# A gated mix of segment attention and a GLU on one core: token gates as VectorE row sums, the second x tile by transposing DMAs, other first loads, the last tile in halves, and a new order

## The chip, the core and the metric

The kernel runs on one core of a Trainium2 chip. The metric is the device time of one execution in microseconds (us). TensorE is called PE, VectorE DVE, ScalarE ACT, GpSimd POOL, SyncE SP.

## What is computed

Input x has 2048 tokens of 512 features in bfloat16. The result mixes two branches by a gate that each token has:

```python
g = sigmoid((x * gate_w).sum(-1, keepdims=True))   # one gate per token
a = A(x)      # 32 heads of 16, 4 segments of 512 tokens: causal softmax attention inside a segment,
              # plus a linear memory of the segments before it (phi(q) @ M, / phi(q) @ z), mixed by
              # sigmoid(beta) per head, then @ wo
b = (gelu(x @ w_gate) * (x @ w_up)) @ w_down        # inner width 1792
out = g * a + (1 - g) * b
```

## The kernel before

All weights stay in SBUF. The work goes by segments s = 0 to 3 of 512 tokens. Each piece of work is a task with a name; its instructions belong to one engine. The list `ORDER` at the end of the file holds all names in one sequence, written out by hand; each engine runs its own tasks in the order of that list and waits for data, with semaphores that the `Emitter` derives from what each instruction reads and writes. A digit behind a colon is the PSUM bank (four banks of 512 float32 columns, `psD`), a letter `a` or `d` says whether ACT or DVE empties the bank. An engine never overtakes: what stands behind a waiting instruction waits too. SP's queue, which issues nearly all DMAs, is such a sequence as well.

The names, with s the segment and t a quarter of the 512 features or of the tokens:
- `ld_x0_*` load the natural x of segment 0; `xtr` turns 128x128 blocks of it on PE and `xev` empties them into `xT` (feature on the partition; three buffers). Segment 1 goes the same way; segments 2 and 3 come as transposing DMAs (`ld_x2_*`, `ld_x3_*`, four each, line 343).
- `K`, `Q`, `V` are projections (four 128x128 by 512 matmuls each, line 452), with `Kev`, `Qev`, `Vev` emptying them and `kpada`, `kpadb` laying K out in halves.
- `st` fills the four banks `psX` with scores (line 586); a segment has 18 fills, lettered A to E; `exp` (ACT, line 592) turns them into `pt`, `msk` (POOL) applies the mask; `pv` multiplies with V (line 628); `tp`, `pvp`, `ot` (DVE) turn, scale and turn back into `oT`.
- `vsh` and `ktr` are DMAs that shift V between partition halves and turn phi(K); `phk`, `phq` make phi; `mz`, `mzacc` write the memory, `nz`, `nd`, `nzp`, `ndp` read it.
- `G`, `U` are the GLU's two projections (14 blocks each), emptied by `Gev` and `gelu` or by `gd` (ACT) and `h` (DVE, line 690); `out` is the down projection (line 703), `wo` the output projection (line 715); `wev` scales the former by 1 - g, `oev` (line 718) adds the latter times g, `dma` stores a tile of 128 tokens. `ost` and `wds` have two buffers each.
- The gates: `gate_w` is loaded as four rows, turned on PE (`gwtr`) and copied (`gwev`). `gate{s}` is 16 matmuls of one column each (line 427) into a bank; `gz` clamps, `gr` takes the exponential, `go` makes g and 1 - g (`gtok`, `omgt`).

At the start, `warm1` runs eight matmuls on zeros. The queues then hold, on SP: x0's first half, the first half of `wk`, `wq` in two halves, `gate_w`, `wv`, x1 in halves, `w_gate` in halves, `beta`; on ACT: x0's second half and the second half of `wk`.

Of the kernel before, what the change touches and what calls it, by code (L numbers as in the profile page):

```python
# [246 lines left out]
def _build(es, nc, A_x, A_wq, A_wk, A_wv, A_wo, A_beta, B_w_gate, B_w_up, B_w_down, gate_w, out):  # L247
# [173 lines left out]
    def gates(s):  # L421
        sl = Slot()
        c = slice(4 * s, 4 * s + 4)
        mm = []
        for q in range(4):
            for kb in range(4):
                mm.append(I(lambda e, q=q, kb=kb: e.matmul(
                    BK[sl.i][:, q:q + 1], xT[s % R_XT][:, kb, q * 128:(q + 1) * 128], gatew[:, kb:kb + 1],
                    start=(kb == 0), stop=(kb == 3)), [("xT", s % R_XT, kb), ("gatew",)], [bk(sl)]))
# [262 lines left out]

    def outputs(s):
        for qt in range(4):
# [19 lines left out]
            so = Slot()  # L714
            one(f"wo{s}_{qt}", PE, 4 * T_MM, [I(lambda e, kb=kb, q=q, so=so: e.matmul(  # L715
                BK[so.i][:, :], oT[:, kb, q], wo[:, kb, :], start=(kb == 0), stop=(kb == 3)),
                [("oT", kb), ("wo",)], [bk(so)]) for kb in range(4)], opens=True)
            one(f"oev{s}_{qt}", DVE, 0.66, [I(lambda e, so=so, gt=gt, wi=wi, oi=oi: e.scalar_tensor_tensor(  # L718
                out=ost[oi][:, :], in0=BK[so.i][:, :], scalar=gtok[:, gt:gt + 1], in1=wds[wi][:, :],
                op0=ALU.mult, op1=ALU.add), [bk(so), ("gtok", s), ("wds", wi)], [("ost", oi)])])  # L720
            one(f"dma{gt}", SP, 0.5, [I(lambda e, gt=gt, oi=oi: e.dma_start(out[0, gt * 128:(gt + 1) * 128, :], ost[oi][:, :]),
                                        [("ost", oi)], [("out", gt)], dma_sem=sem(f"s_out{gt}"))], lat=2.0)

    def head_gates():
# [7 lines left out]
        one("gwtr", PE, T_TR, [I(lambda e: e.transpose(BKbf[sg.i][:, 0:4], gw4, ident[0:4, 0:4]),
                                 [("gw4",), ("omem", 0), ("ident",)], [bk(sg)])], opens=True, bias=30.0)
# [196 lines left out]
```

## Time and profile before

| | |
|---|---|
| runs | 274.26, 274.30, 274.33 us (median 274.3) |
| span of the profiled execution, first to last instruction | 272.5 us |
| profiled execution's own time | not given beside its span; the runs lie 1.8 us above the span |
| granted TensorE clock | 1.000 |
| PE, DVE, ACT, POOL busy | 265.6, 210.4, 206.6, 98.9 us |
| gate matmuls on PE, line 427 | 64, in four blocks |
| turns of x on PE, line 759 | 32 |
| landing of `wk`, first and second half | 6.45 us, 7.16 us |
| first K matmul | 6.54 us |
| read from HBM, written | 8.66 MB, 2.10 MB |

Busy time is the time in which an engine has at least one instruction under way. Matmuls overlap in the array, so PE's busy time says little; starts of consecutive matmuls say more. The chain of waits follows the last instruction back to whatever released each step. A DMA's landing is the time at which its semaphore is raised. All times count from the first instruction.

### The profile page before, as it was taken

How to read it: one execution, taken by the hardware profiler on the slowest of the kernel's cores; microseconds unless marked ns; L12 is line 12 of the kernel's file. 1: busy time of each engine (PE TensorE's matmuls, PEld its weight loads, DVE VectorE, ACT ScalarE, POOL GpSimd, SP SyncE). 2: the span in 40 equal slices, each digit the busy share in tenths (PEclk: the TensorE clock that was granted, in tenths of full speed). 3: DMA queues.
4: the chain of work that ended last, by engine and by line, in shares of the span. 5: the costliest groups of instructions: out<-in, count | busy, mean ns of one | idle time of the engine just before them, and what ended most of it. 6: DMA issues, size and time to landing. Idle time of an engine off the chain costs nothing.

```text
span 272.5 us, 6260 instructions
## 1 busy us (share of the span) xinstructions
PE 265.6 (97%) x2641; PEld 115.5 (42%) x2641; DVE 210.4 (77%) x398; ACT 206.6 (76%) x171; POOL 98.9 (36%) x151
## 2 busy tenths in 40 slices
PE   6999999989999999999999999999999999999995
...
GB/s 230 276 152 182 122 221 156 0 4 33 0 117 158 30 19 19 2 4 19 0 2 2 67 53 0 2 61 61 22 4 0 0 2 2 22 19 2 39 2 78
DMA packets 21812, 14.90 MB, mean 55 GB/s; under 512 B 11800, under 2 KB 20760, under 8 KB 21784
## 3 DMA queue, kind: packets, MB, share of 16 engines
...
q14 instruction: 7, 0.06, 0.1%
HBM read 8.66 MB, written 2.10 MB: 39 GB/s over the span
## 4 chain that ended last, share of the span: by engine, by line
PE 85%; DVE 11%; DMA 2%; issue 1%; ACT 0%; ACTq 0%
PE psD L452 46%; PE psD L703 16%; PE psX L586 8%; PE psD L628 6%; PE psD L715 5%; DVE gb L690 2%; DMA wk<-in_A_wk_dram 2%; DVE ob L639 1%; PE psD L553 1%; DVE phk L466 1%; PE psD L533 1%; PE psD L522 1%; DVE oT L647 1%; DVE phq L466 1%; DVE ob L645 1%
## 5 line engine op out<-in xcount | busy, mean ns | idle before, releaser
L592 ACT ACTIVATE pt<-psX 128x2048 bf16<-128x2048 f32 x72 | 135.1, 1877 | 36.9 <-PE psX L586 35.7
L598 POOL TENSOR_TENSOR pt<-pt,ctri 128x256 bf16<-128x256 bf16 x128 | 94.4, 742 | 157.5 <-ACT pt L592 142.4
L452 PE MATMUL psD<-xT,wu 128*128 128x512 bf16 x224 | 54.8, 380 | 0.7 <-DVE gb L690 0.7
L452 PE MATMUL psD<-xT,wg 128*128 128x512 bf16 x224 | 53.2, 380 | 0.3 <-DVE kT L446 0.3
L703 PE MATMUL psD<-wd,gb 128*128 128x512 bf16 x224 | 53.2, 380 | 0.1
L690 DVE TENSOR_TENSOR gb<-psD,gb 128x512 bf16<-128x512 f32 x56 | 37.4, 681 | 10.3 <-PE psD L452 10.1
L507 DVE STREAM_TRANSPOSE tT<-psD 128x512 f32<-128x512 f32 x47 | 32.3, 703 | 10.1 <-PE psD L628 6.7
L452 PEld LDWEIGHTS psD<-xT,wg 128*128 128x128 bf16 x224 | 21.0, 98 | 26.0 <-issue 1.5
L703 PEld LDWEIGHTS psD<-wd,gb 128*128 128x128 bf16 x224 | 20.6, 98 | 25.4 <-issue 2.6
L452 PEld LDWEIGHTS psD<-xT,wu 128*128 128x128 bf16 x224 | 20.0, 98 | 26.5 <-issue 3.2
L586 PE MATMUL psX<-qT,kD 32*128 32x192 bf16 (+7 forms) x512 | 28.6, 287 | 0.0
L639 DVE SCALAR_TENSOR_TENSOR ob<-tT,gq,rc 128x256 bf16<-128x256 f32 x32 | 18.4, 575 | 1.1
L628 PE MATMUL psD<-pt,vnat 64*17 64x128 bf16 (+7 forms) x512 | 18.9, 283 | 0.0
L586 PEld LDWEIGHTS psX<-qT,kD 32*128 32x128 bf16 x512 | 8.3, 92 | 24.8 <-issue 9.3
L628 PE MATMUL psD<-pt,vsh 64*17 64x128 bf16 (+7 forms) x512 | 18.2, 283 | 0.0
L452 PE MATMUL psD<-xT,wk 128*128 128x512 bf16 x64 | 16.5, 380 | 1.4 <-DMA wk<-in_A_wk_dram 1.3
L673 ACT ACTIVATE gb<-psD 128x512 bf16<-128x512 f32 x28 | 15.2, 597 | 2.1 <-PE psD L452 1.9
L452 PE MATMUL psD<-wv,xT 128*128 128x512 bf16 x64 | 16.5, 380 | 0.0
L452 PE MATMUL psD<-xT,wq 128*128 128x512 bf16 x64 | 16.3, 380 | 0.0
L715 PE MATMUL psD<-wo,oT 128*128 128x512 bf16 x64 | 16.1, 380 | 0.0
L718 DVE SCALAR_TENSOR_TENSOR ost<-psD,gtok,wds 128x512 bf16<-128x512 f32 x16 | 11.9, 742 | 5.3 <-PE psD L715 4.8
L628 PEld LDWEIGHTS psD<-pt,vnat 64*17 64x17 bf16 x512 | 11.5, 86 | 9.0 <-issue 5.5
...
## 6 DMA issues: line engine op xcount, KB each, us to landing
...
```

Of the source, the lines that this page charges most:

```text
L452: one(name, PE, n * T_MM, [I(lambda e, i=i: e.matmul(BK[sl.i][:, :], lhs(i), rhs(i), start=(i == 0), stop=(i == n - 1)), reads(i), [bk(sl) ...
L507: one(f"tp{name}", DVE, 0.605, [I(lambda e, sl=sl, ti=ti: e.transpose(tT[ti][:, :], BK[sl.i][:, :]), [bk(sl)], [("tT", ti)])], bias=bias)
L586: ins.append(I(lambda e, t=t, kb=kb, ncol=ncol, c0=c0, g=g: e.matmul(XALL[:, g * 512 + c0:g * 512 + c0 + ncol], kD[b][32 * g:32 * g + 32, ...
L592: one(f"exp{s}_{name}", ACT, 2048 * 0.000833 + 0.05, [I(lambda e: e.activation(pt[slot][:, :, :], xin, ACTF.Exp, scale=ATT_SCALE), [("X",) ...
L598: ins.append(I(lambda e, mv=mv: e.tensor_tensor(mv, mv, cm, ALU.mult), [("pt", slot), ("causal",)], [("pt", slot)]))
L628: ins.append(I(lambda e, kb=kb, slot=slot, c0=c0, n=n, g=g, r0=r0, sl=banks[j], va=va: e.matmul(BK[sl.i][32 * g:32 * g + 17, 64 * kb:512], ...
L639: I(lambda e, ti=ti, ri=ri, t=t, j=j, dst=dst: e.scalar_tensor_tensor(out=dst, in0=t_rows(ti), scalar=gq[:, 2 * t + j:2 * t + j + 1], in1= ...
L673: t = one(f"gd{s}_{ft}", ACT, 0.485, [I(lambda e, gi=gi, f=f, sl=sl: e.activation(gb[gi][:, f, :], BK[sl.i][:, :], ACTF.Gelu_apprx_tanh), ...
L690: one(f"h{s}_{ft}", DVE, 0.605, [I(lambda e, sl=sl, gi=gi, f=f: e.tensor_tensor(gb[gi][:, f, :], BK[sl.i][:, :], gb[gi][:, f, :], ALU.mult ...
L703: mm.append(I(lambda e, fb=fb, gi=gi, f=f, q=q, sl=sl: e.matmul(BK[sl.i][:, :], gb[gi][:, f, q], wd[:, fb, :], start=(fb == 0), stop=(fb = ...
L715: one(f"wo{s}_{qt}", PE, 4 * T_MM, [I(lambda e, kb=kb, q=q, so=so: e.matmul(BK[so.i][:, :], oT[:, kb, q], wo[:, kb, :], start=(kb == 0), s ...
L718: one(f"oev{s}_{qt}", DVE, 0.66, [I(lambda e, so=so, gt=gt, wi=wi, oi=oi: e.scalar_tensor_tensor(out=ost[oi][:, :], in0=BK[so.i][:, :], sc ...
```

## The change

- Gates: instead of PE matmuls over `xT`, DVE multiplies natural x by `gate_w`, laid out on all partitions (`gwb`), and sums along the row: two instructions with an accumulated output for each half segment (`gs`), then `gm` clamps. Segment 0 takes the natural x that is in SBUF; the others load it again in halves (`ld_n`) into one buffer `xn`. `gwtr`, `gwev` and the gate matmuls are gone.
- Segment 1 of x comes by four transposing DMAs, which wait for `wv`; its natural load, its turns and its evictions are gone.
- First loads: `wk` in four quarters and `wq` in two halves, alternating between SP's queue and ACT's. The turns of x0 are split by halves of its rows (`xp`).
- K of segment 0 is made two column blocks at a time, with the input block outermost.
- A small exponential (`table`) on ACT at the start.
- The last tile of 128 tokens goes through `wo`, `oev` and `dma` in two column halves, by way of `junk`.
- The whole list is another sequence, with other banks and other engines for some evictions (`wev`: 6 on DVE and 10 on ACT instead of 12 and 4).

The diff, cut; of the list only the start, one middle part and the end are shown:

```diff
...
-    gatew = sb("gatew", [P, 4])
+    gwb = sb("gwb", [P, 512])
+    xn = sb("xn", [P, 2, 512])
+    junk = sb("junk", [P, 512])
+    gzr = sb("gzr", [P, 16], F32)
     betab = sb("betab", [P, 8])
...
-    gw4, ball = omem[0:4, 0, 0:P], omem[:, 1, 0:H]
-    stage = (R_PT - 1, R_PT - 2)
+    ball = omem[:, 1, 0:H]
+    stage = R_PT - 1
...
-    def ld_xt(s):
+    def ld_xt(s, wait):
         for kb in range(4):
             load(f"x{s}_{kb}", SP, lambda e, kb=kb: e.dma_start_transpose(
                 xT[s % R_XT][:, kb, :], A_x[0, s * 512:(s + 1) * 512, kb * 128:(kb + 1) * 128]),
-                [("xT", s % R_XT, kb)], issue=1.31, lat=3.0, wait=[("ld", "wo")], ranked=False)
-
-    def ld_xp(s, h, eng, wait=()):
-        ld_w(f"x{s}_{h}", eng, pt[stage[s]][:, halves[h], :],
-             A_x[0, s * 512:(s + 1) * 512, :].rearrange("(q p) d -> p q d", p=P)[:, halves[h], :],
-             [("xs", s, h)], 0.25, wait)
-
-    ld_xp(0, 0, SP)
-    ld_xp(0, 1, ACT)
-    ld_w("wk0", SP, wk[:, halves[0], :], wsrc(A_wk)[:, halves[0], :], [("wk", 0)], 0.25)
-    ld_w("wk1", ACT, wk[:, halves[1], :], wsrc(A_wk)[:, halves[1], :], [("wk", 1)], 0.25)
-    ld_w("wq0", SP, wq[:, halves[0], :], wsrc(A_wq)[:, halves[0], :], [("wq", 0)], 0.25)
-    ld_w("wq1", SP, wq[:, halves[1], :], wsrc(A_wq)[:, halves[1], :], [("wq", 1)], 0.25)
-    ld_w("gw", SP, gw4, gate_w.rearrange("(kb p) -> kb p", p=P), [("gw4",)], 0.01, ["x0_0"])
+                [("xT", s % R_XT, kb)], issue=1.31, lat=3.0, wait=[("ld", wait)], ranked=False)
+
+    for h, eng in ((0, SP), (1, ACT)):
+        ld_w(f"x0_{h}", eng, pt[stage][:, halves[h], :],
+             A_x[0, 0:512, :].rearrange("(q p) d -> p q d", p=P)[:, halves[h], :], [("xs", h)], 0.25)
+    for kb, eng in ((0, SP), (1, ACT), (2, SP), (3, ACT)):
+        ld_w(f"wk{kb}", eng, wk[:, kb, :], wsrc(A_wk)[:, kb, :], [("wk", kb)], 0.125)
+    for h, eng in ((0, SP), (1, ACT)):
+        ld_w(f"wq{h}", eng, wq[:, halves[h], :], wsrc(A_wq)[:, halves[h], :], [("wq", h)], 0.25)
     ld_w("wv", SP, wv[:], wsrc(A_wv), [("wv",)], 0.5, ["x0_1"])
     ld_w("beta", SP, ball, A_beta.partition_broadcast(P), [("ball",)], 0.02, ["wk0"])
-    ld_xp(1, 0, SP, ["wk0", "wk1"])
-    ld_xp(1, 1, SP, ["wq0"])
-    ld_w("wg0", SP, wg[:, halves[0], :], wgr[:, halves[0], :], [("wg", 0)], 0.9, ["wq1"])
-    ld_w("wg1", SP, wg[:, halves[1], :], wgr[:, halves[1], :], [("wg", 1)], 0.9, ["wv"])
-    ld_w("wu0", SP, wu[:, halves[0], :], wur[:, halves[0], :], [("wu", 0)], 0.9, ["x1_1"])
-    ld_w("wu1", SP, wu[:, halves[1], :], wur[:, halves[1], :], [("wu", 1)], 0.9, ["wg0"])
-    ld_w("wd0", SP, wd[:, 0:HFT, :], wdr[:, 0:HFT, :], [("wd", 0)], 0.9, ["wg1"])
+    ld_w("gwb", SP, gwb[:, :], gate_w.partition_broadcast(P), [("gwb",)], 0.125, ["wk0"])
+    ld_w("wg0", SP, wg[:, halves[0], :], wgr[:, halves[0], :], [("wg", 0)], 0.9, ["wk3"])
+    ld_w("wg1", SP, wg[:, halves[1], :], wgr[:, halves[1], :], [("wg", 1)], 0.9, ["wq0"])
+    ld_xt(1, "wv")
+    ld_w("wu0", SP, wu[:, halves[0], :], wur[:, halves[0], :], [("wu", 0)], 0.9, ["wg0"])
+    ld_w("wu1", SP, wu[:, halves[1], :], wur[:, halves[1], :], [("wu", 1)], 0.9, ["wg1"])
+    ld_w("wd0", SP, wd[:, 0:HFT, :], wdr[:, 0:HFT, :], [("wd", 0)], 0.9, ["x1_3"])
     ld_w("wd1", SP, wd[:, HFT:NFT, :], wdr[:, HFT:NFT, :], [("wd", 1)], 0.9, ["wu0"])
     ld_w("wo", SP, wo[:], wsrc(A_wo), [("wo",)], 0.5, ["wu1"])
-    ld_xt(2)
-
+    ld_xt(2, "wo")
...
+    one("table", ACT, 1.3, [I(lambda e: e.activation(rcm[:, 0:8], warm[:, 0:8], ACTF.Exp), [("warm",)], [("rcm",)])])
...
     def gates(s):
-        sl = Slot()
         c = slice(4 * s, 4 * s + 4)
-        mm = []
-        for q in range(4):
-            for kb in range(4):
-                mm.append(I(lambda e, q=q, kb=kb: e.matmul(
-                    BK[sl.i][:, q:q + 1], xT[s % R_XT][:, kb, q * 128:(q + 1) * 128], gatew[:, kb:kb + 1],
-                    start=(kb == 0), stop=(kb == 3)), [("xT", s % R_XT, kb), ("gatew",)], [bk(sl)]))
-        one(f"gate{s}", PE, 0.45, mm, opens=True, bias=30.0)
-        one(f"gz{s}", DVE, 0.2, [I(lambda e: e.tensor_scalar(gz[:, c], BK[sl.i][:, 0:4], ZMAX, None, ALU.min),
-                                   [bk(sl)], [("gz", s)])], bias=30.0)
+        for h in range(2):
+            xs, k = (pt[stage][:, halves[h], :], ("xs", h)) if s == 0 else (xn[:, :, :], ("xn",))
+            if s > 0:
+                ld_w(f"n{s}_{h}", SP, xn[:, :, :],
+                     A_x[0, s * 512:(s + 1) * 512, :].rearrange("(q p) d -> p q d", p=P)[:, halves[h], :],
+                     [("xn",)], 0.25, ["wo"])
+            one(f"gs{s}_{h}", DVE, 1.4, [I(lambda e, q=q, xs=xs: e.scalar_tensor_tensor(
+                out=junk[:, :], in0=xs[:, q % 2, :], scalar=1.0, in1=gwb[:, :], op0=ALU.mult, op1=ALU.mult,
+                accum_out=gzr[:, 4 * s + q:4 * s + q + 1]), [k, ("gwb",), *([("pt", stage)] if s == 0 else [])],
+                [("junk",), ("gzr", s, q)]) for q in (2 * h, 2 * h + 1)])
+        one(f"gm{s}", DVE, 0.2, [I(lambda e: e.tensor_scalar(gz[:, c], gzr[:, c], ZMAX, None, ALU.min),
+                                   [("gzr", s, q) for q in range(4)], [("gz", s)])])
         one(f"gr{s}", ACT, 0.2, [I(lambda e: e.activation(gr[:, c], gz[:, c], ACTF.Exp), [("gz", s)], [("gr", s)])],
             bias=30.0)
         one(f"go{s}", DVE, 0.6, [
...
     def project(s):
         b, b3 = s % 2, s % R_XT
+        if s == 0:
+            kb2 = {}
+            for t in (0, 1):
+                kb2[t], kb2[t + 2] = pair = Slot(), Slot()
+                one(f"K0_{t}", PE, 8 * T_MM, [I(lambda e, t=t + 2 * j, i=i, sl=pair[j]: e.matmul(
+                    BK[sl.i][:, :], wk[:, i, t * 128:(t + 1) * 128], xT[0][:, i, :], start=(i == 0), stop=(i == 3)),
+                    [("xT", 0, i), ("wk", i)], [bk(pair[j])]) for i in range(4) for j in range(2)], opens=True)
         for t in range(4):
-            sl = dense(f"K{s}_{t}", lambda i, t=t: wk[:, i, t * 128:(t + 1) * 128], lambda i: xT[b3][:, i, :],
-                       lambda i: [("xT", b3, i), ("wk", i // 2)], 4)
+            sl = kb2[t] if s == 0 else dense(f"K{s}_{t}", lambda i, t=t: wk[:, i, t * 128:(t + 1) * 128], lambda i: xT[b3][:, i, :],
+                       lambda i: [("xT", b3, i), ("wk", i)], 4)
             evict(f"Kev{s}_{t}", kT[:, t, :], sl, [], [("kT", 0, t)])
             kin = kT[:, t, :].rearrange("p (m c) -> p m c", c=64)
...
             one(f"h{s}_{ft}", DVE, 0.605, [I(lambda e, sl=sl, gi=gi, f=f: e.tensor_tensor(
                 gb[gi][:, f, :], BK[sl.i][:, :], gb[gi][:, f, :], ALU.mult), [bk(sl), ("g", gi, f)], [("g", gi, f)])])
+    outs = []
+
     def outputs(s):
         for qt in range(4):
             gt = 4 * s + qt
...
                 (DVE, 0.66, [I(lambda e, sl=sl, gt=gt, wi=wi: e.tensor_scalar(
                     wds[wi][:, :], BK[sl.i][:, :], omgt[:, gt:gt + 1], None, ALU.mult),
                     [bk(sl), ("omgt", s)], [("wds", wi)])])], L_DVE)
...
+            parts = (("", slice(0, 512)),) if gt < 15 else (("a", slice(0, 256)), ("b", slice(256, 512)))
+            for pi, (sfx, c) in enumerate(parts):
+                so, w = Slot(), c.stop - c.start
+                one(f"wo{s}_{qt}{sfx}", PE, 4 * T_MM / len(parts), [I(lambda e, kb=kb, q=q, so=so, c=c, w=w: e.matmul(
+                    BK[so.i][:, 0:w], oT[:, kb, q], wo[:, kb, c], start=(kb == 0), stop=(kb == 3)),
+                    [("oT", kb), ("wo",)], [bk(so)]) for kb in range(4)], opens=True)
+                dst, dk = (ost[oi], ("ost", oi)) if not sfx else (junk, ("junk", pi))
+                one(f"oev{s}_{qt}{sfx}", DVE, 0.66, [I(lambda e, so=so, gt=gt, wi=wi, dst=dst, c=c, w=w: e.scalar_tensor_tensor(
+                    out=dst[:, c], in0=BK[so.i][:, 0:w], scalar=gtok[:, gt:gt + 1], in1=wds[wi][:, c],
+                    op0=ALU.mult, op1=ALU.add), [bk(so), ("gtok", s), ("wds", wi), *([("junk",)] if sfx else [])], [dk])])
+                outs.append(f"s_out{gt}{sfx}")
+                one(f"dma{gt}{sfx}", SP, 0.5, [I(lambda e, gt=gt, dst=dst, c=c: e.dma_start(
+                    out[0, gt * 128:(gt + 1) * 128, c], dst[:, c]), [dk], [("out", gt, pi)],
+                    dma_sem=sem(outs[-1]))], lat=2.0)
     def head_gates():
...
-        sg = Slot()
-        one("gwtr", PE, T_TR, [I(lambda e: e.transpose(BKbf[sg.i][:, 0:4], gw4, ident[0:4, 0:4]),
-                                 [("gw4",), ("omem", 0), ("ident",)], [bk(sg)])], opens=True, bias=30.0)
-        one("gwev", DVE, 0.1, [I(lambda e: e.tensor_copy(gatew[:, :], BKbf[sg.i][:, 0:4]), [bk(sg)], [("gatew",)])],
-            bias=-150.0)
...
-    def turn_x(s):
-        xs = pt[stage[s]]
-        for kb in range(4):
-            sl = Slot()
-            one(f"xtr{s}_{kb}", PE, 4 * T_TR, [I(lambda e, q=q, kb=kb, sl=sl: e.transpose(
-                BKbf[sl.i][:, q * 128:(q + 1) * 128], xs[:, q, kb * 128:(kb + 1) * 128], ident[:, :]),
-                [("xs", s, q // 2), ("pt", stage[s]), ("ident",)], [bk(sl)]) for q in range(4)], opens=True)
-            task(f"xev{s}_{kb}", [
-                (ACT, 0.477, [I(lambda e, kb=kb, sl=sl: e.activation(xT[s][:, kb, :], BKbf[sl.i][:, 0:512], ACTF.Copy),
-                                [bk(sl)], [("xT", s, kb)])]),
-                (DVE, 0.335, [I(lambda e, kb=kb, sl=sl: e.tensor_copy(xT[s][:, kb, :], BKbf[sl.i][:, 0:512]),
-                                [bk(sl)], [("xT", s, kb)])])], L_DVE)
-
-    turn_x(0)
-    turn_x(1)
+    for kb in range(4):
+        sl = Slot()
+        for h in range(2):
+            one(f"xp{kb}_{h}", PE, 2 * T_TR, [I(lambda e, q=q, kb=kb, sl=sl: e.transpose(
+                BKbf[sl.i][:, q * 128:(q + 1) * 128], pt[stage][:, q, kb * 128:(kb + 1) * 128], ident[:, :]),
+                [("xs", h), ("pt", stage), ("ident",)], [bk(sl)]) for q in (2 * h, 2 * h + 1)], opens=(h == 0))
+        task(f"xev0_{kb}", [
+            (ACT, 0.477, [I(lambda e, kb=kb, sl=sl: e.activation(xT[0][:, kb, :], BKbf[sl.i][:, 0:512], ACTF.Copy),
+                            [bk(sl)], [("xT", 0, kb)])]),
+            (DVE, 0.335, [I(lambda e, kb=kb, sl=sl: e.tensor_copy(xT[0][:, kb, :], BKbf[sl.i][:, 0:512]),
+                            [bk(sl)], [("xT", 0, kb)])])], L_DVE)
+
     head_gates()
     for s in range(NSEG):
         if s == NSEG - 1:
-            ld_xt(s)
+            ld_xt(s, "wo")
         project(s)
         if s > 0:
             memory_read(s)
...
-            for gt in range(16):
-                e.wait_ge(sem(f"s_out{gt}"), 16)
+            for name in outs:
+                e.wait_ge(sem(name), 16)
...
 ORDER = """
...
-ld_x0_0 ld_x0_1 ld_wk1 warm0 ident consts causal1 causal0 masks warm1:0 ld_wk0 ld_wq1 ld_wq0 ld_gw ld_wv ld_x1_0
-ld_x1_1 ld_wg1 ld_wg0 ld_beta xtr0_2:1 xtr0_3:2 xtr0_1:3 xtr0_0:0 vones0 xev0_3:d xev0_2:a xev0_1:a xev0_0:d K0_0:1
-Kev0_0:d K0_2:2 kpada0_0 kpadb0_0 Q0_0:3 Qev0_0:a Kev0_2:a gwtr:0 K0_1:1 st0_0A exp0_0A V0_2:3 K0_3:2 gwev Kev0_1:d
-kpada0_1 Kev0_3:a xtr1_1:0 V0_1:1 st0_0B Vev0_2:d phka0_0 exp0_0B phkb0_0 kpada0_3 xev1_1:d phka0_2 Vev0_1:d Q0_2:3
...
-pv3_3:12 wev3_0:d wev3_1:a tp3_d31 tp3_d30 pvp3_31 pvp3_30 ot3_3 dma10 dma11 out3_2_0:3 out3_3_0:0 out3_3_1 out3_3_2
-wo3_0:2 wo3_1:1 oev3_0 oev3_1 dma12 dma13 out3_2_1 out3_2_2 wo3_2:2 wo3_3:1 wev3_2:d wev3_3:a oev3_2 oev3_3 dma14
-dma15
+ident warm0 warm1:0 ld_x0_0 ld_x0_1 ld_wk0 ld_wk2 xp1_0:1 xp0_0:2 xp3_0:3 xp0_1 masks causal0 consts causal1 xp3_1
+xp2_0:0 ld_wk1 ld_wk3 ld_wq0 ld_wq1 xev0_3:a xev0_0:d xp2_1 xp1_1 xev0_1:d xev0_2:a K0_0:23 ld_beta ld_wv Kev0_0:d
+kpada0_0 table K0_1:10 Kev0_1:a Kev0_2:a ld_gwb Q0_0:2 kpadb0_0 betab Q0_1:1 gs0_0 Qev0_0:a Kev0_3:a kpadb0_2 phka0_2
+st0_0A exp0_0A V0_2:3 V0_0:2 Q0_3:0 vones0 gs0_1 causal Vev0_0:d kpadb0_1 Qev0_1:d st0_0B Vev0_2:a exp0_0B phkb0_2
+ld_wg0 ld_x1_1 ld_wg1 Q0_2:3 V0_3:2 G0_2:1 st0_0C exp0_0C Qev0_3:d Qev0_2:d kpada0_2 Gev0_2:d phkc0_2 phka0_0 phkb0_0
+ld_x1_2 ld_x1_0 ld_x1_3 V0_1:0 V1_1:3 G0_0:1 Vev1_1:d Vev0_3:d kpadb0_3 kpada0_1 Gev0_0:d st0_0D Q1_3:3 G0_1:2 V1_2:1
+Vev0_1:a phkc0_0 exp0_0D st0_0E Qev1_3:d ktr0_2 ld_wu1 vsh0_01 Vev1_2:d G1_5:0 K1_2:3 Kev1_2:d G0_3:1 kpada1_2
+Gev0_3:d Gev1_5:d Gev0_1:a exp0_0E bexp gph st0_1A vsh0_21 vsh0_00 exp0_1A G1_4:2 V1_0:3 K1_0:1 msk0_0C msk0_0A
...
+exp1_0D st1_0E exp1_0E out0_1_2 wo0_1:3 V2_3:0 wev0_1:d gs1_1 gm1 oev0_1 nzp1 st1_1A out0_2_0:1 out0_2_1 wo0_0:2
+out0_2_2 G1_8:3 oev0_0 wev0_2:d ndp1_1 phka2_0 Vev2_3:d G1_13:2 exp1_1A G1_10:1 G1_7:0 gelu1 gd1_13 gd1_8 gd1_10 gd1_7
+G1_9:2 nd1_2:3 gd1_9 msk1_0D ndp1_0 ld_n2_0 vsh1_20 ktr1_2 tp1_m2 ndp1_2 phka2_2 vsh1_21 ld_x3_1 st1_1B msk1_1A
+msk1_0E dma0 dma1 vsh1_01 ld_x3_0 msk1_0C msk1_0A pv1_0:10 exp1_1B V2_2:2 out0_3_0:3 tp1_d00 Vev2_2:d tp1_d01 U1_9:1
...
+wev2_2:a st3_3B msk3_2A msk3_2D msk3_2E msk3_2C pv3_2:12 tp3_d20 pvp3_11 wo2_2:3 out3_1_0:0 exp3_3B msk3_3B st3_3C
+exp3_3C go3 tp3_d21 ot3_0 out3_1_1 out3_1_2 out3_0_0:1 st3_3D pvp3_21 ot3_1 oev2_2 pvp3_20 dma11 dma10 msk3_3A msk3_3C
+out3_0_1 out3_0_2 exp3_3D wev3_1:a msk3_3D out3_2_0:2 pv3_3:30 ot3_2 wev3_0:d out3_3_0:1 out3_2_1 out3_2_2 out3_3_1
+tp3_d30 pvp3_30 tp3_d31 pvp3_31 ot3_3 wo3_0:3 oev3_0 dma12 wo3_1:0 out3_3_2 oev3_1 wev3_2:a dma13 wo3_3a:3 wev3_3:a
+oev3_3a dma15a wo3_2:2 oev3_2 dma14 wo3_3b:0 oev3_3b dma15b
```

More of the change, by code (lines that the diff above doesn't have):

```diff
@@ L713, in outputs @@
                     [bk(sl), ("omgt", s)], [("wds", wi)])])], L_DVE)
[L714 to L722, printed above, removed]
+            parts = (("", slice(0, 512)),) if gt < 15 else (("a", slice(0, 256)), ("b", slice(256, 512)))
[12 more added lines that the diff above has]
+                    dma_sem=sem(outs[-1]))], lat=2.0)
     def head_gates():
@@ L841 @@
-st0_0D Qev0_1:a Vev0_0:a betab Vev0_3:d kpadb0_3 kpadb0_1 G1_5:2 Q1_3:0 G0_0:3 Gev1_5:d Qev1_3:d Gev0_0:d exp0_0D bexp
-phkb0_2 st0_0E exp0_0E vsh0_21 ld_wu1 vsh0_00 vsh0_01 vsh0_20 Q0_3:2 Qev0_3:d phkc0_2 ld_wo G0_4:0 K1_3:3 Gev0_2:a
-st0_1A exp0_1A Gev0_4:d Kev1_3:d phkc0_0 ld_x2_3 ktr0_3 ld_wd0 ktr0_1 ld_x2_2 ktr0_2 ld_x2_1 V1_0:2 G0_5:1 msk0_0A
-msk0_0B msk0_0C msk0_0D msk0_0E pv0_0:03 Gev0_5:a st0_1B kpada1_3 Vev1_0:d gq tp0_d00 K1_1:1 tp0_d01 Kev1_1:d G0_6:2
-G1_4:0 exp0_1B Gev1_4:a st0_1C exp0_1C V1_1:3 Q1_2:1 G0_1:0 Vev1_1:a kpada1_1 kpadb1_1 kpadb0_2 Qev1_2:d kpada0_2
@@ L856 @@
-tp0_d31 exp1_0A phqb1_2 gr0 st1_0B exp1_0B vsh1_20 ktr1_3 ld_x3_1 ld_wd1 vsh1_01 ktr1_2 ktr1_0 ld_x3_0 ld_x3_3 vsh1_21
-ktr1_1 vsh1_00 ld_x3_2 G1_2:2 Q2_1:1 V2_3:0 st1_0C tp0_d30 phqc1_2 Qev2_1:a exp1_0C pvp0_30 ot0_2 Vev2_3:d Gev1_2:d
-pvp0_31 out0_1_0:3 V2_2:1 nz1:0 st1_0D Vev2_2:a exp1_0D out0_1_1 out0_1_2 nd1_1:2 st1_0E nd1_2:1 tp1_z go0 nzp1
-wev0_1:d tp1_m1 G1_3:0 nd1_0:3 out0_0_0:2 phka2_2 tp1_m0 Gev1_3:d tp1_m2 ot0_3 ndp1_2 exp1_0E st1_1A msk1_0A msk1_0B
-msk1_0C msk1_0D msk1_0E exp1_1A out0_0_1 out0_0_2 pv1_0:30 st1_1B gelu1 wev0_0:d ndp1_1 tp1_d01 phqa2_0 wo0_1:1
```

96 lines of the change are left out of this document (48 added, 48 removed).

## The prediction

> **What bounds the kernel now.** I read the page first (engines, then slices), then the chain of waits by stretches, then busy time by windows, last the groups by form and the time line of the two ends.
>
> ```profile
> PE 265.6 (97%) x2641; PEld 115.5 (42%) x2641; DVE 210.4 (77%) x398; ACT 206.6 (76%) x171; POOL 98.9 (36%) x151
> PE   6999999989999999999999999999999999999995
> ```
>
> TensorE (PE) looks full except in the first slice, at 60 to 80 us and at the end. Busy time overlaps, so I counted starts as well. The chain gives the pitches: sixteen 512-column matmuls in 3.48 us (0.217 each), a block of 64 `pv` matmuls 1.10, a fill of XALL 0.33. PE's instructions in the order of the list at those pitches, plus 0.1 us wherever a fill or `pv` follows dense work, leave only 4.5 us of idle PE: 1.5 before the first K and 0.24 inside it, 0.92 at 60.8 us, 0.23 at 63.6, 0.71 at 78.4 to 79.0, 0.17 at 259.6, the rest crumbs. So a microsecond of PE work taken away is a microsecond gained, unless another engine is late. [...]
>
> ```profile
> 1.33 5.82 DMA wk<-in_A_wk_dram
> 7.16 0.05 issue
> 7.20 2.33 PE psD L452 x10
> ```
>
> The chain's head: the first projection waits for `wk`'s second half (issued on ScalarE's queue, landed 7.16 us). Two K matmuls run before that.
>
> ```profile
> 71.03 1.20 DVE gb L690 x2
> 72.23 0.55 DVE phq L462
> 72.77 1.61 DVE phk L466
> 74.38 0.60 DVE gb L690
> ```
>
> From 54.9 to 79.0 us the chain runs mostly through VectorE (DVE): this is the one stretch where PE waits for it. Its window rows (columns: PE, PEld, DVE, ACT, POOL busy; clock; DMA) from fill st0_3A to st1_1A:
>
> ```profile
> 62.60:74.70 12.10, 12.02 (x149) 5.29 (x148) 10.26 (x19) 10.60 (x9) 4.89 (x6) 1.00 0.08 19
> 74.70:90.40 15.70, 15.44 (x159) 6.40 (x158) 15.17 (x28) 12.37 (x11) 8.71 (x11) 1.00 0.62 131
> ```
>
> DVE has 25.4 us of work in 27.8.
>
> **PE work removed.** The chain's pitches again:
>
> ```profile
> 49.20 0.38 PE psD L427 x16
> 12.77 0.22 PE psD L759 x4
> 9.53 0.11 PE psD L732
> ```
>
> Four gate blocks of 0.38 (1.5), four turns of x1 of 0.22 (0.9), the turn of `gate_w` 0.11 and the 0.1 around it (0.2): **-2.6 us**. All of it stands between dense work, so it is on the path. The column halves of the last tile are eight 256-column matmuls for four of 512: no change.
>
> **Head.** `wk` comes in four quarters, two on SP's queue, two on ScalarE's. ScalarE's queue carries the same 512 KB of x0 and `wk` as before, so I leave the last quarter's landing at 7.16; the others, by halving the old waits (x0 3.95 and 4.24, `wk` 6.45 and 7.16), at about 5.2, 5.7 and 6.45. The new K0_0 takes kb outermost over two column blocks, so six of 16 matmuls can be over by 7.2 instead of two: 4 x 0.217 = 0.9. The turns of x0 just make it: GpSimd now writes `ident` ahead of `warm` (0.44 and 0.25 us, rows of the first us), so `warm1` starts at 1.75 instead of 1.07, its 3.06 us end at 4.8, the turns at 5.7, the last eviction for i=2 at 6.6, and i=0, 1, 2 run at 5.9, 6.4, 6.85. I take **-0.8**. If ScalarE's queue is slower (wk3 at 8.0) it is 0; if faster, -1.2. Its evictions and `exp0_0A` come 0.7 us later, but so much PE work (8 matmuls more, 1.7 us) is then done that nothing waits. SP now holds `beta`, `wv`, `gwb`, `wg0` behind a wait for wk0 (5.2): `wv` is issued at about 5.9 instead of 4.34. It was last of 2 MB in one stream (9.69) and stays so at about 9.9; V0_2 wants it at 11.5. `gs0_0` waits for `gwb`, right behind `wv`, about 10.3, when DVE comes to it; `kpadb0_2` to `Qev0_1` queue behind it.
>
> The x1 transposes: the first waits for `wv`; `wg1` is queued behind its issue, so goes at 11.4 instead of 9.71. With two more issues of 1.27 us (row of `xT` transposes) the last is issued at about 14.4 and lands 2.6 to 4.8 us later (the range of the old eight), 17.0 to 19.2. V1_1, the first reader, comes at about 18.6 and its last kb at 19.2; G0_2 wants `wg1` at 16.8, which I put at 16.2 (0.9 MB took 2.3 us behind another). So 0 to 2 us; I take **+0.2**, near the low end since seven of eight transposes landed in under 4 us.
>
> **VectorE.** Sixteen gate sums of 128x512 come in. No row has this form; the nearest below is the plain product, above it the three-operand form at twice the width:
>
> ```profile
> L645 DVE TENSOR_TENSOR ob<-ob,omem 128x512 bf16<-128x512 bf16 x12 | 5.9, 496 | 0.1
> L466 DVE SCALAR_TENSOR_TENSOR phk<-kT,phk 128x1024 bf16<-128x1024 bf16 x6 | 8.2, 1370 | 0.0
> ```
>
> So 0.5 to 1.37 us each; I take half the latter, 0.65 to 0.69, as the same form with the same columns: 16 x 0.66 = 10.6. [...] No run here shows the form. Out go four evictions of x1 (4 x 0.42), `gwev` 0.16, and six of twelve `wev` (6 x 0.75), which go to ScalarE; six plain evictions (6 x 0.68) come over. DVE: 210.4 + 10.6 - 1.9 - 4.5 + 4.1 = 218.7, or 81% of 270. ScalarE stays within 1 us; `table` is one exponential of 8 columns (0.2 by the row of `gr`) while it would wait for the first K.
>
> On average that is hidden under PE; where it isn't is read by stage. I counted both lists between the same fills at the same prices.
> - st0_2A to st0_3A (24.6 us, PE work 23.6): DVE loses 1.1, the two K1/phi pieces ahead of U0 are gone; walking the new list by banks I find no wait where there was 0.96. **-0.9**.
> - st0_3A to st1_1A: DVE +2.2 (`gs1_1` and others), 27.6 of work, against PE 26.0. DVE sets it: 27.3 (my walk, with waits at st0_3D and before nz1 for `phqc1_2`) to 28.5 where it was 27.8. PE saves 0.8 here and keeps little: **+0.5** against the PE sum.
> - 145 to 196 us: DVE 44.6 in 51.2 becomes 45.0 in 47.1 (PE work moved out), 95% full: 0 to 2 us of waiting, **+0.5**, as the 93% stretch above cost 1.0.
>
> SP's moves: six natural loads of x (0.45 us an issue) in one buffer, each but the first held until the sums before it are done. Behind n2_0 wait vsh1_20, ktr1_2 and, after dma0 and dma1, vsh1_01, which pv1_0 reads. From the end of wo0_0: eviction 0.95, two output issues 0.7, vsh to landing 2.1, 3.8 us; PE has 5.8 us of listed work there. Cost 0; 1 to 3 us if DVE falls over 2 us behind.
>
> **End.**
>
> ```profile
> 267.36 1.89 PE L715 MATMUL psD<-wo,oT 128*128 128x512 bf16 x8
> 268.42 1.61 DVE L718 SCALAR_TENSOR_TENSOR ost<-psD,gtok,wds 128x512 bf16<-128x512 f32 x2
> ```
>
> After the last matmul DVE has a 0.75 eviction, then the store. Now a half (0.48, the 256-wide row of L639), but it queues behind the whole oev3_2: **-0.2** (0 to -0.3). PE's cover for the chain pv3_3 to ot3_3 (4.1 us) is the same four pieces' worth.
>
> Sum: -2.6 - 0.8 + 0.2 - 0.9 + 0.5 + 0.5 - 0.2 = -3.3. The profiled span is 272.5; the median of the runs is 274.3, so 1.8 us lie around the span, which I keep: span 269.2, time **271.0**.
>
> **Rivals.**
> 1. *VectorE becomes the bound (slower).* If a sum with its accumulation costs as much as the 1024-wide row, 1.3 us, DVE gets 10 us more. Stage by stage the excess over PE grows by 1.9 (st0_0A to st0_1A, two pairs), 1.7 (st0_3A to st1_1A), 1.5 (145 to 196), 0.5 (196 to 219), and DVE two and more us behind opens the vsh1_01 wait, 1.5: 271.0 + 7.1 = 278.1. It turns to slower at about 1.0 us a sum. For it: DVE already leads the chain from 54.9 to 79. Against: the same form at half width should be half. Chance 0.17.
> 2. *x1 and wg come late.* If wk0 lands at 6.45 as the half did, every issue behind it moves by 1.3 us and the last transpose lands at 20.5 to 21.4: 2 to 3 us at G0_2 and V1_1, time 273.5. Chance 0.15.
> 3. *The PE saving is swallowed.* The stages at 93 to 95% each lose 1 us more than I took and the head gains nothing: 271.0 + 2 + 0.8 + 0.5 = 274.3, no change. Chance 0.06.
>
> **Numbers.** The forecast has 0.62, its own range 269.5 to 272.6 (head 0 or -1.2, sums 0.5 us, stage waits 0 to 2). A change of 0.2% is 0.55 us, about what runs of this kernel can tell. Faster: forecast and rival 2, 0.77; same 0.06; slower 0.17. The range goes from 269.0 up to 274.8, past rivals 2 and 3, leaving rival 1 out.
>
> **What would show it.** PE busy near 263 us; `wk` gone from the chain after 7.2 us with six matmuls before; the 128x512 sums at 0.6 to 0.7 us; fill st1_1A at about 89.5 us instead of 90.4; no wait of PE on `xT` transposes over 0.5 us; DVE busy about 219. I am wrong if the sums take 1 us, if PE waits for `wg` or `xT` between 16 and 21 us by more than 1 us, or if the chain after 90 us runs through DVE for more than a few us.

## The result and the profile after

| | before | changed |
|---|---|---|
| median of 19 runs each | 274.33 us (273.37 to 275.6) | 275.50 us (274.56 to 277.5) |
| ratio | | 1.0043, 95% interval 1.0027 to 1.0058 |
| span of the profiled execution | 272.5 us | 274.1 us |
| first PE instruction; last matmul's start to span end | 1.07; 3.6 us | 1.73; 3.2 us |
| PE waits between its listed pieces, at the prediction's pitches | 4.3 us | 8.2 us |

The change is 1.2 us slower, where 3.3 us less were forecast. The span's +1.6 adds up: 2.6 of PE work gone, 0.7 later start, 3.9 more waiting, 0.4 less behind the last matmul. The page of the changed kernel, engines, PE by slices, chain by engines; the last line is the chain before:

```profile
PE 260.8 (95%) x2526; PEld 114.1 (42%) x2564; DVE 218.0 (80%) x426; ACT 207.0 (76%) x172; POOL 95.7 (35%) x151
PE   7989998999999999999999999899999999999995
PE 64%; DVE 21%; ACT 4%; issue 4%; DMA 4%; SPq 0%; DVEq 0%
...
PE 85%; DVE 11%; DMA 2%; issue 1%; ACT 0%; ACTq 0%
```

PE's count is 38 short of PEld's (matmul records missing), so its busy time reads low. The chain is the line to look at: before it read PE 85%, DVE 11%; now a fifth of the span runs through DVE. The chain of the first 26 us (start, length, what) says where that begins:

```profile
1.32 3.39 DMA wk<-in_A_wk_dram
...
5.58 7.34 DMA gwb<-in_gate_w_dram
...
13.02 0.71 DVE junk L427 x2
...
24.75 1.04 PE psD L452 x4
```

`wk` hands over to the load of `gate_w`; from its landing at 12.92 us to 24.7 us DVE leads, with the first two sum pairs and all that queues behind them. Among that is `vones0`, a memset of 0.17 us (15.44) that stands behind `gs0_0`: ACT's Vev0_2 waited for it until 15.70 us, and PE's Q0_2 waited for the bank that Vev0_2 empties (PE's time line; in brackets the idle time before and who ended it):

```profile
16.36 1.04 PE L452 MATMUL psD<-xT,wq 128*128 128x512 bf16 x4 [0.53 <-ACT vnat L445]
17.61 1.04 PE L452 MATMUL psD<-wv,xT 128*128 128x512 bf16 x4 [0.21 <-DVE vnat L446]
```

Two more places, in the chains of 38 to 47 and of 168 to 176 us:

```profile
41.64 1.12 DVE junk L427 x2
...
42.79 1.04 DVE junk L427 x2
43.83 0.60 DVE qT L446
44.43 0.61 DVE gb L446
...
45.08 1.15 PE psD L635 x49
```

```profile
170.08 0.60 DVE gb L697
170.68 1.10 DVE omem L547
171.78 0.68 DVE kD L487
172.46 0.64 DVE tT L514
...
173.14 0.60 PE psD L452 x2
```

At 41.6 us the pair `gs1_0` stands ahead of two evictions whose banks `pv0_1` needs (0.82 and 0.52 us of PE waiting); at 172 us V3_3 waits 1.1 us for the bank that `tp2_d01` frees. The windows that answer to the stage rows of the prediction (the first is st0_2A to st0_3A, the second st0_3A to st1_1A, the third st2_0A to st3_0A):

```profile
40.71:66.19 25.48, 24.22 (x194) 10.46 (x197) 19.01 (x38) 21.54 (x20) 7.23 (x12) 1.00 0.39 95
66.19:93.36 27.17, 26.02 (x287) 11.10 (x291) 24.66 (x50) 20.82 (x16) 10.05 (x13) 1.00 0.13 28
148.22:197.13 48.91, 46.83 (x546) 20.03 (x552) 44.12 (x87) 38.96 (x27) 20.89 (x32) 1.00 0.16 37
```

### The profile page after: what moved, and what is told of

Read it like the earlier page. It is cut to its first block, busy times and chain, and to the rows that moved or that the text cites. A ratio compares the mean times of both kernels' runs of the same rounds, so it can differ in the third digit from the quotient of the medians.

```text
span 274.1 us, 6113 instructions
## 1 busy us (share of the span) xinstructions
PE 260.8 (95%) x2526; PEld 114.1 (42%) x2564; DVE 218.0 (80%) x426; ACT 207.0 (76%) x172; POOL 95.7 (35%) x151
## 4 chain that ended last, share of the span: by engine, by line
PE 64%; DVE 21%; ACT 4%; issue 4%; DMA 4%; SPq 0%; DVEq 0%
PE psD L452 36%; PE psD L712 11%; PE psX L593 6%; PE psD L635 5%; PE psD L726 4%; DVE tT L514 3%; DMA gwb<-in_gate_w_dram 3%; ACT pt L599 2%; DVE kD L487 2%; DVE junk L427 2%; DVE ob L646 2%; DVE gb L446 2%; DVE oT L654 2%; DVE gb L697 1%; DMA wk<-in_A_wk_dram 1%
## 5 line engine op out<-in xcount | busy, mean ns | idle before, releaser
L605 POOL TENSOR_TENSOR pt<-pt,ctri 128x256 bf16<-128x256 bf16 x128 | 91.2, 723 | 164.6 <-ACT pt L599 160.2
L452 PE MATMUL psD<-xT,wu 128*128 128x512 bf16 x214 | 53.1, 379 | 1.2 <-issue 0.8
L712 PE MATMUL psD<-wd,gb 128*128 128x512 bf16 x215 | 52.4, 380 | 1.6 <-issue 1.1
L452 PE MATMUL psD<-xT,wg 128*128 128x512 bf16 x215 | 51.8, 380 | 1.2 <-issue 0.6
L635 PE MATMUL psD<-pt,vnat 64*17 64x128 bf16 (+7 forms) x512 | 19.2, 283 | 0.8 <-DVE qT L446 0.8
L635 PE MATMUL psD<-pt,vsh 64*17 64x384 bf16 (+7 forms) x512 | 18.4, 283 | 0.1
L646 DVE SCALAR_TENSOR_TENSOR ob<-tT,gq,rc 128x256 bf16<-128x256 f32 x32 | 17.2, 538 | 1.1
L452 PE MATMUL psD<-wv,xT 128*128 128x512 bf16 x59 | 15.2, 380 | 1.9 <-DVE tT L514 1.0
L730 DVE SCALAR_TENSOR_TENSOR ost<-psD,gtok,wds 128x512 bf16<-128x512 f32 x15 | 11.1, 746 | 6.6 <-PE psD L726 6.4
L726 PE MATMUL psD<-wo,oT 128*128 128x512 bf16 (+1 forms) x66 | 15.7, 367 | 0.3 <-issue 0.2
L717 ACT ACTIVATE wds<-psD,omgt 128x512 f32<-128x512 f32 x10 | 6.8, 684 | 11.1 <-PE psD L726 8.1
```

The lines of the kernel that those rows point to most:

```text
L452: one(name, PE, n * T_MM, [I(lambda e, i=i: e.matmul(BK[sl.i][:, :], lhs(i), rhs(i), start=(i == 0), stop=(i == n - 1)), reads(i), [bk(sl) ...
L605: ins.append(I(lambda e, mv=mv: e.tensor_tensor(mv, mv, cm, ALU.mult), [("pt", slot), ("causal",)], [("pt", slot)]))
L635: ins.append(I(lambda e, kb=kb, slot=slot, c0=c0, n=n, g=g, r0=r0, sl=banks[j], va=va: e.matmul(BK[sl.i][32 * g:32 * g + 17, 64 * kb:512], ...
L646: I(lambda e, ti=ti, ri=ri, t=t, j=j, dst=dst: e.scalar_tensor_tensor(out=dst, in0=t_rows(ti), scalar=gq[:, 2 * t + j:2 * t + j + 1], in1= ...
L712: mm.append(I(lambda e, fb=fb, gi=gi, f=f, q=q, sl=sl: e.matmul(BK[sl.i][:, :], gb[gi][:, f, q], wd[:, fb, :], start=(fb == 0), stop=(fb = ...
L726: one(f"wo{s}_{qt}{sfx}", PE, 4 * T_MM / len(parts), [I(lambda e, kb=kb, q=q, so=so, c=c, w=w: e.matmul(BK[so.i][:, 0:w], oT[:, kb, q], wo ...
```

## The experiments

Theory **V**: the sums load VectorE too much. **H**: the start (first loads, `gate_w`, warm-up) is late. **O**: the new sequence itself puts DVE work at places where PE waits for it. Ratios are to the kernel before, with 95% intervals. The first four start from the changed kernel.

```diff
 e1_no_sums
-    one(f"gs{s}_{h}", DVE, ...)          # 16 sums; gate_w and x are still loaded
+    cn.append(I(lambda e: e.memset(gzr[:], 0.0), ...))
```

> The changed kernel without the sixteen gate sums on VectorE (left out: the gates are constants; the six natural loads of x stay). Its profile has 8.2 us of PE waits where the kernel before has 4.3. Theory V (the sums fill VectorE, and PE waits for evictions behind them): nearly all of the surplus goes, 3 to 3.5 us less, about 272.2. Theory H (it is the start: late gate_w, late warm-up): only the waits between 12 and 25 us go, 1.2 to 1.4 us, about 274.2. Theory O (the new sequence has these waits whatever the gates are): within 0.5 us of 275.5.

274.25 us, 1.0005 (0.9978 to 1.0032): the number that H had forecast, between V's and O's. The waits at nz1, G1_7 and V3_3 stay as they were (0.57, 0.45, 1.11 us), those at V0_3 and pv0_1 go. So the sums cost 1.0 us by the ratios (1.25 by the medians) where they stand, and even without one of them the new sequence only equals the old, with 2.6 us less for PE to do.

```diff
 e2_gates_pe
-    gs, ld_n, gwb
+    gate0..3, gwtr, gwev as before, in the new sequence
```

> The changed kernel with the gates on PE again as before (turn of gate_w, four blocks of 16 one-column matmuls where the clamps stood), everything else as changed. PE gets 1.6 + 0.7 us more work (blocks, turn and the spaces around them). Theory V: the waits fall by 3 to 3.5, so about 1 us faster than the changed kernel, 274.4. Theory O: 277.5 or more. Theory H: 1.2 less and 2 more, 276.3.

277.33 us, 1.0111 (1.0087 to 1.0134): 1.8 us over the changed kernel. That is close to O's number (277.5 or more). Even where they stand, sums beat gates on PE; V in its plain form is out.

```diff
 e3_warm_first:   -ident warm0 ...            +warm0 ident ...
 e4_gwb_first:    -ld_wv ld_gwb (waits wk0)   +ld_wq1 ld_gwb (no wait)
```

> The changed kernel with GpSimd's zeros for the warm-up written before the identity instead of after it (two names exchanged in the list). The warm-up then starts at 1.07 instead of 1.73 us and the turns of x0 at about 4.4, warm. Theory H: the first K moves from 6.8 to 5.9 and the end by 0.6 to 0.9 us. Theory V: VectorE still waits for gate_w until 12.9 us and leads from there, so under 0.3 us is left of it.

> The changed kernel with the broadcast of gate_w issued on SP's queue right behind wq, ahead of beta and wv, with no wait. It should land at about 8.4 instead of 12.9 us, so that VectorE does not sit idle for 2.2 us before its first sum. Theory H: the PE waits at 16.4, 17.6 and 24.7 us (1.4 in all) go, 1.0 to 1.4 us less, about 274.3. Theory V: VectorE makes this up only in part, 0.3 to 0.8 less. Theory O: nothing.

275.53 us, 1.0053 (1.0032 to 1.0075), and 275.68 us, 1.0051 (1.003 to 1.0071). With e3 the fill st0_0A came 1.55 us earlier and st0_1A only 0.40: 1.15 us more of waiting stood between them. With e4 `gate_w` landed at 9.36 instead of 12.92 us and st0_1A came 0.44 earlier, 0.25 of it already at st0_0A; in between, G0_2 waited for `wg1` (18.41). Each cover hides the next.

```diff
 e5_head (changed kernel)
-ident warm0 | ld_x1_1 ld_wg1 | V1_1 G0_0 | gs0_0 at 13 us, gs0_1 at 15, gs1_0 at 42
+warm0 ident | ld_wg1 ld_x1_1 | G0_0 V1_1 | ld_gwb ld_n0_0 behind x1; gs0_0 at 32 us, gs0_1 at 47, gs1_0 at 61
```

> The changed kernel with its first 28 us and its first three sums rearranged: warm0 ahead of ident on POOL; wg1 issued ahead of the transposed x1; gate_w's load and the first tile's natural x behind them, and the first tile's sums at 33 us and 50 us where VectorE sat idle for 1.9 and 3.8 us, instead of at 13 and 15 us; the third sum pair (gs1_0) at 64 us instead of 41.6; V1_1 behind G0_0. In the changed kernel G0_2 starts at 18.46 us, at which wg1 lands (18.43), in both head experiments as well (18.46, 18.41), so that either edit alone had a cover left. If gate_w, the warm-up and wg1 cover each other: the stage st0_1A starts at 26.5 instead of 28.74, and the 0.82 and 0.52 us of waits at 44.5 and 46.2 us go: 275.5 - 2.2 - 1.3 = 272.0. If a fourth cover holds (the transposed x1, last landed at 19.9): only the 1.3 at 44 to 46 us go, 274.2. If TensorE's waits only move on to the next place: 275.5.

272.75 us, 0.9941 (0.9925 to 0.9957), 2.75 less than the changed kernel and faster than before. St0_1A stood at 27.2 and both waits at 44 to 46 us were gone.

```diff
 e6_dve_moves (changed kernel, VectorE's sequence)
-ot0_2 .. phqc1_2 | ndp1_1 phka2_0 Vev2_3 | pvp2_00 h2_6 ndp2_2 kpadb3_3 tp2_d01 | wev3_1:a ot3_2 wev3_0:d
+phqc1_2 ot0_2 .. | Vev2_3 ndp1_1 phka2_0 | h2_6 ndp2_2 tp2_d01 pvp2_00 kpadb3_3 | wev3_0:a wev3_1:a ot3_2
```

> The changed kernel with five VectorE operations moved in its sequence, no work left out: phqc1_2 ahead of ot0_2 (nz1 to nd1_1 waits 0.57 us behind it), Vev2_3 ahead of ndp1_1 (G1_7 waits 0.45), ndp2_2 and tp2_d01 ahead of pvp2_00 (V3_3 waits 1.11 for its bank), ot0_3 behind tp1_m0, and wev3_0 on ScalarE ahead of wev3_1 (out3_3_0 waits 0.45). If the new sequence's own waits cost time (theory O): 275.5 - 2.6 = 272.9. If VectorE's load is what counts, not its order (V): its work is the same, 275.5, with the waits elsewhere. In between if the moves push other evictions back by half of it: 274.2.

275.45 us, 1.0048 (1.0026 to 1.007): no gain, the number that was set for V. Two waits only moved on, which its time line shows for the first (PE's weight loads):

```profile
92.23 0.55 PEld L726 LDWEIGHTS psD<-wo,oT 128*128 128x128 bf16 x4 [1.93 <-DVE tT L514]
```

The phi piece had gone ahead, and wo0_1's loads now stood idle for 1.93 us, until `tp1_z`, left behind three pads and `go0`; pv2_1 waited 0.67 for `tp2_m3`. Its start shows the covers once more: in this profile st0_0A came 1.13 us earlier than in the changed kernel's, st0_1A only 0.09.

```diff
 e7_before_sums, e10_before_sums_2 (kernel before)
-    gate0..3, gwtr, gwev
+    gs in places where DVE sat idle; ld_n, ld_gwb (e10: behind the vsh stores)
```

> The kernel before, in its old sequence, with only the gates changed: the four gate matmul groups and gate_w's turn are gone from TensorE (4 x 0.40 + 0.2 = 1.8 us), and 16 sums stand on VectorE at places where it sat idle for 1 to 4 us before. If a sum in an idle place is free and the new sequence is to blame (O): 274.3 - 1.8 = 272.5. If VectorE's 11.6 us of sums cost as such (V): 274.3 or more, up to 276. If TensorE's saving is swallowed by the next VectorE wait: 274.3.

> e7_before_sums (the kernel before with only the gates as sums) with three loads at other places in SP's queue: gate_w and the first natural half behind the four vsh stores instead of ahead of them, the second natural half ahead of wu0 instead of behind it. In e7 pv0_0 waited 1.10 us for a vsh store, and a sum at 45 us waited 3.6 us for its data until 48.7 us and kept mzacc0_2 and h0_4 behind it. If the loads cost what was saved: 274.2 - 1.7 = 272.5. If the sums themselves cost it: 274.5 again.

e7: 274.58 us, 1.0009 (0.999 to 1.0028). e10: **272.39 us, 0.9945** (0.9925 to 0.9966), 1.85 less than before where PE lost 1.8 us of work. Sums in the old sequence give all of it; three loads at the wrong places in SP's queue take all of it away again.

```diff
 e8_before_tail:          +wo3_3a wo3_3b, oev, dma in halves
 e11_before_x1:           -ld_xp(1, ..), turn_x(1)      +ld_xt(1, "wv") behind ld_beta
 e13_before_first_loads:  +wk in quarters, wq on two queues, K0_0 and K0_2 together
```

> The kernel before with only the last tile's output in two column halves (wo3_3, its eviction and its store). The time from the last matmul's end to the span's end was 3.7 us before and 3.2 in the changed kernel. If the halves do that: 274.3 - 0.5 = 273.8. If the new sequence of the last matmuls did it: 274.3, or 274.5 by the extra instructions.

> The kernel before with only the second tile of x brought by four transposing DMAs (behind beta's load) instead of natural loads and 16 turns on TensorE with four evictions. TensorE has 4 x 0.22 = 0.9 us less and the evictions' engines 2 us less; in the changed kernel the four transposes landed at 15.7 to 19.9 us. Here x1 is first read at 20 us (G1_5). If they land by then: 274.2 - 0.9 = 273.3. If late by 1 us or wg is pushed back behind them: 274.2 to 275.

> The kernel before with only the first loads of the change: wk in four quarters and wq in two halves, alternating between SP's queue and ACT's, and the first two K pieces made together with the input block outermost. The prediction gave the head 0.8 us, from the profiled landing of wk at 6.45 and 7.16 us. If that landing is the usual one: 274.2 - 0.8 = 273.4. In the profiles of e7 and e8, with the same loads, wk landed at 5.36 to 5.83 us and the first K ran at 5.88 instead of 6.51; if that is the usual one, the turns of x0 end with it and there is nothing to gain: 274.2, or up to 0.5 above for the later st0_0A.

274.19 us, 0.9995 (0.9981 to 1.0008); 274.01 us, 0.9992 (0.9976 to 1.0007); 274.23 us, 0.9996 (0.9979 to 1.0013). None of the three parts gives anything that can be measured; for x1 the interval ends at a gain of 0.66 us, short of the 0.9 of PE work that is gone; why is open. In e13's profile the last quarter of `wk` landed at 7.17 us and K ran from 6.07, but then Q0_0 waited 0.51 us for `wq` (8.52), and st0_0A stood at 10.61, where it had stood at 10.54.

```diff
 e14_head_no_sums_moved (changed kernel)
+warm0 ident | ld_wg1 ld_x1_1 | G0_0 V1_1        # e5_head without its sums and loads for them
```

> Part of e5_head: the changed kernel with warm0 ahead of ident, wg1 issued ahead of the transposed x1, and V1_1 behind G0_0; gate_w's load and all sums stay where the change put them. e5_head won 2.75 us in all. If wg1 and the warm-up are what the head's 1.5 us hang on: 275.5 - 1.5 = 274.0. If VectorE, held by gate_w until 12.9 us and by two sum pairs, covers them (V0_3 and Q0_2 waited 1.0 us there, and 1.3 us fell at 44 to 46 us behind gs1_0): 275.5 to 275.0, and the 2.75 us of e5_head are the sums' places.

276.03 us, 1.0065 (1.0037 to 1.0094). So warm-up and `wg1` alone give nothing while the first sums and the load of `gate_w` stay: the first K ran 0.8 us earlier (6.02) and st0_1A 0.1 (28.64), and the chain of the first 26 us is again

```profile
5.93 6.60 DMA gwb<-in_gate_w_dram
...
12.63 0.71 DVE junk L427 x2
```

How those 3.3 us (276.03 to 272.75) divide between `gate_w`'s landing and the sums' own 1.4 us a pair was not tried one by one; e4 says that the landing alone is not enough. Nor does e14 show that warm-up and `wg1` give nothing once the sums are moved: the sums were not moved alone, and e1, without any sum but with these two as the change has them, stayed behind e5 by 1.5 us in the medians and 0.5 in the profiled spans.

```diff
 e9_head_and_moves (e5_head):      moves of e6, and  +nz1 tp1_z kpadb2_1 kpada2_3 | tp2_m3 kpadb3_3 phqa3_0
 e12_two_more_moves (e9):          +tp1_z go0 wev0_0 kpadb2_1 | kpada0_2 Vev0_3 Gev0_2
```

> e5_head with the VectorE moves of e6_dve_moves, mended by its trace: there wo0_1 came to wait 1.93 us for tp1_z, which then stood behind three pads and go0, and pv2_1 0.67 us for tp2_m3; here tp1_z stands ahead of the pads and tp2_m3 ahead of kpadb3_3 and phqa3_0. e5_head still waits 0.56 (nz1), 0.25, 0.45 (G1_7), 1.12 (V3_3) and 0.3 (end). If those are places of the sequence alone (O): 272.75 - 2.4 = 270.3. If VectorE owes that work anyway and any order only moves the wait, as in e6: 272.7. Half: 271.5.

> e9_head_and_moves with go0 and wev0_0 ahead of three pads on VectorE (V2_3 waited 1.36 us at 88.5 for the bank that wev0_0 frees) and Vev0_3 ahead of Gev0_2, into an idle stretch of 0.8 us at 17 us (Q1_3 and V1_2 waited 0.3 each for evictions behind it). If these waits too belong to the places in the sequence: 271.1 - 0.9 - 0.3 = 269.9. If VectorE now owes the work anyway: 271.1.

e9: 271.13 us, 0.9896 (0.9875 to 0.9918). e12: **270.98 us, 0.9890** (0.9873 to 0.9907), with a span of 269.3. The moves that won nothing in e6 won 1.6 us by the medians (1.2 by the ratios) on top of e5 and with the waits behind them moved as well; which of the two it took was not tried. In e12 the wait before st1_1A fell from 1.05 to 0.14 us, and 0.75 came up inside pv1_0, which now waited for a `vsh` store. The page of e9, engines and chain, and its chain of the first 26 us (excerpt):

```profile
PE 264.3 (98%) x2564; PEld 114.5 (42%) x2564; DVE 216.6 (80%) x425; ACT 207.4 (77%) x173; POOL 98.2 (36%) x151
PE 91%; DVE 6%; ACT 1%; issue 1%; DVEq 0%; POOL 0%; POOLq 0%
...
4.65 1.57 PE psD L765 x16
6.22 3.71 PE psD L474 x16
...
11.99 2.70 PE psD L450 x12
```

DVE does the same sums (216.6 us busy, 80%), and PE leads from the start: DVE can carry this load, and what it cost, it cost by its places.

## Why the prediction was wrong, step by step

Two steps failed: the head's gain of 0.8 us was not there, and the waits of PE behind added and moved DVE pieces, which the walk put at nothing or at 0.5 us a stage, grew by 3.9 us. Term by term:

- **PE is the bound; 2.6 us go.** Right as a size: PE lost 77 instructions, and e10 turned 1.8 us of them into 1.85 us of time. That the best version stands 3.0 us below the kernel before, near the forecast's sum, is luck: it got there by moves that the forecast did not have. As a rule, "a microsecond of PE work taken away is a microsecond gained, unless another engine is late" held for the gates in the old sequence, not in full for x1 (e11), and in the new one its condition failed: PE's waits rose from 4.3 to 8.2 us.
- **Head, -0.8: the step that failed first.** It came from one landing of `wk` at 7.16 us in one profiled execution. In e7, e8, e10 and e11, with the same loads, `wk` landed by 5.88, and in e7 and e8 the first K ran at 5.88 and 5.84, when the turns are done: there the term has nothing to win. In e13's profile `wk` was late again, and what the quarters won there went into the wait for `wq`. In the changed kernel the quarters did land earlier than assumed (6.67 the last), but the turns of x0, put to end at 5.7 us, began at 5.12 and ran at 0.107 us each instead of 0.056, so the first K ran at 6.82; by 7.2 us two K matmuls had begun, not six. St0_0A was 1.86 us later than before, not 0.7.
- **`gate_w` at 10.3 us, cost 0: mis-sized, and its queue was not priced.** It landed at 12.92 (`wv` 11.16 instead of 9.9). The text named "`kpadb0_2` to `Qev0_1`" behind it and gave that no price; the price was 1.0 us at Q0_2 and V0_3, and it covered most of what else was won at the start (e3, e6, e14). In e5 st0_1A stood 1.5 us earlier and the 1.34 us behind `gs1_0` were gone, which together is about its gain of 2.75.
- **x1 and `wg`, +0.2.** The last transpose landed at 19.93 (17.0 to 19.2 foreseen), `wg1` at 18.43 (16.2). Rival 2 had the lateness in part (its last transpose at 20.5 to 21.4) but not the cause: `wk0` landed at 4.71; `wv` held the first transpose on SP until 11.16 us, and `wg1` stood behind that. It cost no further time, as PE came to G0_2 only at 18.48; it hid part of the gain of e4, where G0_2 then waited for `wg1`.
- **VectorE's sums.** 0.69 us in the median, as foreseen (0.65 to 0.69), and DVE 218.0 us (218.7). Source view of the line:

```profile
L427 DVE SCALAR_TENSOR_TENSOR junk<-xn,gwb x12: 649/692/1177, 41.6 to 214.6; 128x512 bf16<-128x512 bf16 x12
L427 DVE DVE_READ_ACCUMULATOR junk<-xn,gwb x12: 75/80/84, 42.7 to 215.2; 128x1 f32 x12
```

  So rival 1's price (1.0 us a sum or more) did not come as a rule, and its outcome, slower, did: by place, not by load. But three of the sixteen took 1.03 to 1.18 us beside GpSimd, and two of these are the pair `gs1_0`, 2.2 us where 1.4 were counted, just where PE waited.
- **st0_2A to st0_3A, -0.9.** The walk found no wait; there were 1.5 us, 1.34 of them at pv0_1 behind `gs1_0`. The stage took 25.48 us where 24.6 less the gain were expected. The stretch before it, st0_1A to st0_2A, was not walked.
- **st0_3A to st1_1A.** Right: 27.17 us (27.3 by the walk), with the wait for `phqc1_2` at nz1 (0.57). The fill st1_1A stood at 93.36, not 89.5, for what had come before.
- **145 to 196 us, +0.5.** 1.8 us of waits, 1.1 of them in one place (V3_3), where four DVE pieces stood ahead of the one that frees the bank. A share of 95% does not find such a place; the banks of the list do. The prediction's sign for this came: after 90 us the chain ran 28 us through DVE, where it had been 9.
- **End, -0.2.** The span's end came 0.4 us nearer to the last matmul, by the profile; in the time (e8) nothing that can be measured. The queue behind the whole `oev3_2` was as foreseen (time line):

```profile
270.77 0.75 DVE L730 SCALAR_TENSOR_TENSOR ost<-psD,gtok,wds 128x512 bf16<-128x512 f32 x1
271.44 0.48 DVE L730 SCALAR_TENSOR_TENSOR junk<-psD,gtok,wds 128x256 bf16<-128x256 f32 x1
```

As a sum: the parts alone give -1.85 (sums), -0.2, 0 and 0 (x1, tail, first loads), 2.0 us if they add; the change cost 1.2; so its sequence costs about 3.2 us, with what was not tried alone from the old side (the split turns of x0, `ident` ahead of `warm0`). Moving pieces in it won back 4.2 by the ratios (e5, e9, e12), some of that beyond what it had cost.
